# Carrying the sign of a double through a shift: one VectorE step fewer in the conversion of the weights, and new ranks for the planner

## Chip, core and metric

The kernel runs on one NeuronCore of a Trainium2 chip. The metric is the device time of one execution in microseconds (us), as the median of several runs.

Its engines are named as the profile names them: PE (TensorE, matmuls), PEld (PE's weight loads, which overlap its matmuls), DVE (VectorE), ACT (ScalarE), POOL (GpSimd) and SP (SyncE, here a queue that issues DMAs). Each works through its own instructions in the order in which the program was written, and waits on semaphores for the others.

## What is computed

The reference in its essence, for 4 batches, 8 heads, 576 positions, head size 64:

```python
scores = scale * q @ k.T
cum = np.cumsum(np.log(np.clip(f, 1e-4, 1.0)), axis=-1)
scores = np.where(causal, -1e9, scores + cum[:, :, :, None] - cum[:, :, None, :])
attn = softmax(scores) @ v                      # 4 x 8 heads of 576 x 64
x = attn.transpose(0, 2, 1, 3).reshape(2304, 512)
x = ((x @ w_a) * (x @ w_b)) @ w_out             # 512 -> 1536 -> 512
h = x @ w_in                                    # 512 -> 1024
solu = h * softmax(h)
out = (layer_norm(solu) * g_ln) @ w_out2        # 1024 -> 512
```

The weights of both MLPs and `g_ln` are float32 by value, but the conversion in the kernel shows how `moe_w_a`, `moe_w_b`, `moe_w_out`, `moe2_w_in` and `moe2_w_out` arrive: as 64-bit doubles, of which the kernel reads the two 32-bit halves and puts a float32 together by itself.

## The kernel before

**Precision.** PE multiplies a rounded type (fp32r). Every operand is split into a high part (a cast) and a low part (value minus high part), and a product is three matmuls: high by high, low by high, high by low. Casts and subtractions are what ACT, DVE and POOL mostly do.

**Stages.** Attention runs head by head (first the eight heads of batch 0 in two pieces each, then whole heads): transposes (L944), maxima of scores (matmul L1008, mask L1012, DVE's maximum L1032 or L1035), scores (L1082, L1090), exponentials on ACT (L1147, L1210), weighting with v (L1171, L1269), normalising (L1293 to L1325). Between them lie the "up" products (L1401: x by w_a and w_b, 1728 matmuls of 512 or 256 columns), whose results (ACT L1424, DVE L1426) go to DRAM through SP. When attention is over, the rest of the up products follow, then "down" (L1707: groups of 12 matmuls for one of 12 chunks, `down`), then pairs of 128 rows each (`pair`, `rest`): seven products of sums and differences (L1793), softmax and norm, transposes (L1902) and the last product (L1917). A block of down needs its chunk read back (nat), cast by ACT (L1695) and subtracted (L1699), with two buffers for it; when a block's four PSUM banks are full, ACT copies them out (L1716), and the next block may use them. For the first block these copies also have to come after the conversion of `moe2_w_in` (up to L1617 and L1621), whose memory they overwrite. The pair's quarters are then cast (L1757), subtracted (L1761) and combined (L1767).

**Conversion of a weight tile** (`load_cols`), 56 times, 48 of them with 512 columns and 8 with 256. A DMA brings both halves of the doubles into `raw`. Then:

1. L661: ACT (or POOL, L664) multiplies the high half, read as a float32, by 2^-112 (`rebias`).
2. L673 on ACT or L676 on POOL: the low half's top byte becomes the three missing mantissa bits (`three`).
3. L681 on DVE: shift the result of 1 left by three and OR in the three bits.
4. L685 on DVE: AND the high half with the sign bit and OR it in.
5. L690 on DVE for the 8 tiles of `moe2_w_out` alone: times `g_ln`.
6. L703 (ACT or POOL) casts the high part, L708 (DVE or POOL) subtracts for the low part; for `moe2_w_in` the tile goes through L1628 (differences), L1617 (casts) and L1621 (subtractions) first.

28 tiles (w_a, w_b) are converted while attention begins, 12 (`moe_w_out`) around its end, 8 (`moe2_w_in`) before the first pair and 8 (`moe2_w_out`) around it. In this kernel all 56 of step 1 stand on ACT.

**Order.** Nothing in it is written by hand. Every step is an operation with a key and one or two engines that can do it (`op`); `Sched.run` goes through them with a cost for each, gives out buffers and PSUM banks, picks for each engine the earliest that can start (by key among equals) and the engine that would end first, with a lean for each kind. The table `Y` holds the keys, ranks and leans. The list it makes is the program. Where the planner expects PE to be without work for more than `FG` us early in the kernel, `fill` (L1978) puts matmuls on PE whose results nobody uses, for the share `FF` of that gap.

Of the kernel before, what the change touches and what calls it, by code (L numbers as in the profile page):

```python
# [8 lines left out]
F32 = mybir.dt.float32  # L9
# [14 lines left out]
def t_act(n, psum=False):  # L24
    return (0.167 if psum else 0.2) + n / 1200.0


def t_dve(n):
    return 0.153 + n / 960.0
# [42 lines left out]
class Sched:  # L72
# [228 lines left out]
    "T0": 5.7779,  # L301
    "T1": 5.884,
    "TA": 10.92,
    "TF": 18.3671,
    "U0": 3.9329,
    "U1": 3.2704,
    "UF": 2.3238,
    "UL": 1.3336,
    "LEAD": (1.3468, 6.1224),
    "SHRINK": 2.3365,  # L310
    "W0": 39.835,
    "WD0": 3.1123,
    "WN": 4,
    "WD1": 0.0081,
    "WD2": 15.0328,
    "EZ": 9.4388,
    "EO": 19.7242,
    "TE": 28.8271,
    "DL": 0,
    "BIAS": 0.6613,  # L320
    "UO": (7.859, 9.2606, 7.5415),
    "UD": 27.1947,
    "UK": 414.1889,
    "L3": 17,
    "TL": (0.0, 0.0),
    "F1": 255.5172,
    "FG": 0.2449,
    "FF": 0.6945,
# [3 lines left out]
    "YC": 23.0831,  # L332
    "T2": 10.2775,
    "TB": 1,
    "HB": 1,
    "F2": 251.1376,
    "LATE": -0.663,
# [26 lines left out]
    "WIN": 0.0002,  # L364
# [4 lines left out]
def kernel(  # L369
# [228 lines left out]
    def load_cols(src_view, key, dst_hi, dst_lo, wbuf, wparts, tfetch=6.0, scale=None, kind=1,  # L598
# [35 lines left out]
        def wmv():  # L634
            return stage(wm, n)
# [13 lines left out]
        def hi_w():  # L649
# [6 lines left out]
        ab = op([("ACT", t_act(1.1 * n)), ("POOL", 0.18 + 0.00268 * n)], key - 0.6, None,  # L656
                r=[(raw, 0)], w=[(wm, 0)], lean="BA")

        def rebias():
            if ab.eng == "ACT":  # L660
                nc.scalar.activation(  # L661
# [890 lines left out]
    n = m = 0  # L1552
# [475 lines left out]
```

## Time and profile before

| | |
|---|---|
| median of 3 runs | 904.08 us (902.7 to 907.12) |
| the profiled execution: its time | 904.06 us |
| the profiled execution: its span in the trace | 902.3 us |
| PE busy | 886.6 us (98%) |
| DVE busy | 621.1 us (69%) |
| ACT busy | 456.4 us (51%) |
| POOL busy | 150.6 us (17%) |
| L661, L685 (steps 1 and 4 above) | 56 instructions each |

All durations below come from that profiled execution. Busy PE is not the same as useful PE: the filler of L1978 counts as busy, and matmuls are pipelined, so that a record lasts longer than the distance to the next. The chain of waits follows the work back from the last instruction, and each piece of it names what the end waited for at that moment.

### The profile page before, as it was taken

The page shows a single profiled execution, that of the slowest core. Times are in us where ns is not written, and L with a number is a line of the kernel's source. Part 1 is how long each engine was busy: PE and PEld are TensorE (multiplying, and loading weights), DVE is VectorE, ACT ScalarE, POOL GpSimd, SP SyncE. Part 2 cuts the span into 40 slices and gives each one's busy share as a digit, 9 for nine tenths or more (in the row PEclk, how much of TensorE's full clock was granted, in tenths as well). Part 3 has the DMA queues.
Part 4 walks back from the last instruction along what each step waited for, and adds up shares of the span by engine and source line. Part 5 has one row for each costly group of instructions (what it writes and reads, how often), then busy time and mean ns, then how long its engine had stood idle before and what let it go on. Part 6 is the DMA issues. An engine that isn't in the chain of part 4 may idle for free.

```text
span 902.3 us, 14146 instructions
## 1 busy us (share of the span) xinstructions
PE 886.6 (98%) x4968; PEld 758.8 (84%) x4973; DVE 621.1 (69%) x1214; ACT 456.4 (51%) x859; POOL 150.6 (17%) x293
## 2 busy tenths in 40 slices
PE   8999999999999999999999999899999999999997
PEld 5778878999888888888888889788888888888885
DVE  7877767677665567553773425889687678678775
ACT  5867766566556555454552324645334434253232
POOL 5766454243101111111110000000000000000000
PEclk9999999999999999999999999999999999999999
DMA  5465664334233333122563333442110111111101
GB/s 138 105 172 155 183 181 126 89 83 102 66 90 90 89 96 88 52 74 64 194 210 134 117 94 101 130 155 82 59 48 36 47 59 48 44 45 36 42 12 35
DMA packets 110042, 85.00 MB, mean 94 GB/s; under 512 B 69874, under 2 KB 91508, under 8 KB 109972
## 3 DMA queue, kind: packets, MB, share of 16 engines
q1 hardware_dynamic: 107652, 83.43, 32.3%
q10 hardware_dynamic: 2320, 0.68, 0.4%
q8 instruction: 39, 0.64, 0.3%
q14 instruction: 31, 0.25, 0.1%
HBM read 57.38 MB, written 19.55 MB: 85 GB/s over the span
## 4 chain that ended last, share of the span: by engine, by line
PE 92%; DVE 4%; ACT 1%; issue 1%; POOL 0%; DMA 0%; DVEq 0%; ACTq 0%; POOLq 0%
PE ps L1401 33%; PE ps L1707 16%; PE ps L1917 10%; PE ps L1793 9%; PE ps L1269 6%; PE ps L1090 3%; PE ps L1008 3%; PE ps L1171 3%; PE ps L1082 3%; PE ps L944 2%; PE ps L1902 2%; DVE mts L1032 1%; PE ps L1978 0%; PE ps L1050 0%; PE ps L1012 0%
## 5 line engine op out<-in xcount | busy, mean ns | idle before, releaser
L1401 PE MATMUL ps<-xs,wt 128*128 128x256 f32 (+1 forms) x1728 | 323.7, 340 | 0.1
L1401 PEld LDWEIGHTS ps<-xs,wt 128*128 128x128 f32 x1728 | 266.5, 189 | 33.4 <-POOL wt L708 0.5
L1707 PE MATMUL ps<-wt,sets 128*128 128x512 f32 (+1 forms) x420 | 91.0, 371 | 0.0
L1707 PEld LDWEIGHTS ps<-wt,sets 128*128 128x128 f32 x420 | 73.8, 190 | 13.4
L1793 PE MATMUL ps<-wt,xs 128*128 128x512 f32 x306 | 78.8, 394 | 2.6 <-ACT xs L1757 1.6
L1917 PE MATMUL ps<-wt 128*128 128x512 f32 x324 | 79.6, 394 | 1.5 <-ACT wt L1905 1.4
L1426 DVE TENSOR_TENSOR fw<-ps,fw 128x256 f32<-128x256 f32 (+1 forms) x72 | 40.0, 555 | 55.1 <-PE ps L1401 34.4
L1424 ACT COPY fw<-ps 128x256 f32<-128x256 f32 (+1 forms) x72 | 34.5, 479 | 83.3 <-PE ps L1401 80.9
L1917 PEld LDWEIGHTS ps<-wt 128*128 128x128 f32 x324 | 59.7, 188 | 14.7 <-ACT wt L1905 1.8
L1035 DVE CUSTOM_DVE_ANT_0 ps<-ps,cmask 128x512 f32<-128x512 f32 (+4 forms) x105 | 56.5, 555 | 22.1 <-PE ps L1008 19.6
L1793 PEld LDWEIGHTS ps<-wt,xs 128*128 128x128 f32 x306 | 57.4, 190 | 14.9 <-ACT xs L1757 1.8
L1695 ACT CAST wt<-nat 128x512 fp32r<-128x512 f32 (+1 forms) x60 | 34.6, 579 | 69.1 <-PE ps L1707 63.7
L1234 DVE TENSOR_TENSOR pexp<-fw,pexp 128x768 fp32r<-128x768 f32 (+1 forms) x44 | 45.2, 1027 | 33.3 <-ACT pexp L1228 32.6
L1699 DVE TENSOR_TENSOR wt<-nat,wt 128x512 fp32r<-128x512 f32 (+1 forms) x60 | 38.0, 635 | 40.9 <-ACT wt L1695 40.7
L1269 PE MATMUL ps<-pexp,VS 128*128 128x448 f32 (+4 forms) x396 | 64.8, 311 | 0.0
L1269 PEld LDWEIGHTS ps<-pexp,VS 128*128 128x128 f32 x396 | 59.5, 190 | 3.5
L1219 POOL TENSOR_SCALAR_AFFINE_SELECT fw<-fw 128x128 f32<-128x128 f32 (+1 forms) x120 | 34.5, 317 | 150.4 <-ACT fw L1210 150.4
L1082 PE MATMUL ps<-sets 128*128 128x320 f32 (+4 forms) x200 | 49.2, 295 | 0.1
L1210 ACT ACTIVATE fw<-ps 128x768 f32<-128x768 f32 (+1 forms) x48 | 39.6, 836 | 19.0 <-PE ps L1090 15.2
L1090 PE MATMUL ps<-sets 67*128 67x288 f32 (+6 forms) x200 | 48.9, 320 | 0.0
L1008 PE MATMUL ps<-sets 66*128 66x512 f32 (+3 forms) x192 | 44.3, 332 | 2.9 <-DVE mts L1032 1.1
L1293 ACT ACTIVATE xrw<-ps 64x576 f32<-64x576 f32 (+2 forms) x40 | 22.0, 550 | 48.1 <-PE ps L1269 37.8
(190 smaller groups left out, 1485.9 us busy)
## 6 DMA issues: line engine op xcount, KB each, us to landing
gs<-fw SPq DMA_DIRECT2D x36, 256.0 KB
nat<-gs SPq DMA_DIRECT2D x36, 256.0 KB
fw<-in_moe_w_out_dram SPq DMA_DIRECT2D x16, 512.0 KB
sets<-sets SPq DMA_DIRECT2D x48, 144.0 KB
fw<-in_moe_w_a_dram SPq DMA_DIRECT2D x10, 512.0 KB
fw<-in_moe_w_b_dram SPq DMA_DIRECT2D x10, 512.0 KB
gs<-fw SPq DMA_DIRECT2D x36, 128.0 KB
nat<-gs SPq DMA_DIRECT2D x36, 128.0 KB
```

Of the source, the lines that this page charges most:

```text
L1008: nc.tensor.matmul(bank(ms[part], o, w), lhsT=MB(st)[:D + 2, i * P:(i + 1) * P], rhs=SB(st)[:D + 2, k0:k0 + w], start=True, stop=not pm)
L1035: nc.vector.tensor_tensor_reduce(out=x, in0=x, in1=cmask[:n, off:off + w], scale=1.0, scalar=-3.0e38, op0=ALU.add, op1=ALU.max, accum_out= ...
L1082: nc.tensor.matmul(dst, lhsT=SA(st)[:, ks], rhs=MA(st)[:, q0:q1], start=True, stop=False)
L1090: nc.tensor.matmul(dst, lhsT=SB(st)[:depth, ks], rhs=MB(st)[:depth, q0:q1], start=False, stop=True)
L1210: op(("ACT", t_act(n, True)), key + K.rk[4] + 5.5 + 0.9 * i, lambda i=i, n=n, pf=pf: nc.scalar.activation(out=pf(), in_=bank(ss[i], K.base ...
L1234: o.fn = lambda o=o, bh=bh, bl=bl, n=n, pf=pf: ENG[o.eng].tensor_tensor(out=pexp[:, 64 * bl.slot:64 * bl.slot + n], in0=pf(), in1=pexp[:, ...
L1269: nc.tensor.matmul(bank(u, K.uo + q0, q1 - q0), lhsT=V[:, vp], rhs=src[:, o:o + q1 - q0], start=(k_ in K.first and ip == 0), stop=(k_ in K ...
L1401: nc.tensor.matmul(bank(u[m % len(u)], uo[m], n_), lhsT=wv(m, wp, c)[:, kk], rhs=xsv(i, xx, kk), start=(kk == 0 and n == 0), stop=(kk == K ...
L1426: op(("DVE", t_dve(n_)), key - 50.0, lambda: nc.vector.tensor_tensor(out=gtv(), in0=bank(u[-1], uo[1], n_), in1=atv(), op=ALU.mult), r=[(u ...
L1707: nc.tensor.matmul(bank(py, 512 * d, n), lhsT=WO[c][0][:, wp * DM:(wp + 1) * DM][:, ds_], rhs=ghv(gb, gp)[:, :n], start=(c == 0 and i == 0 ...
L1793: nc.tensor.matmul(bank(bk, 0, 512), lhsT=yc(yx, yp)[:, kk], rhs=wi(wx, wp, kk), start=(n == 0), stop=(n == 5))
L1917: nc.tensor.matmul(bank(po, 0, DM), lhsT=zp[:, c], rhs=w2(c, wp), start=(c == 0 and i == 0), stop=(c == NF2 - 1 and i == 2))
```

## The change

Step 4 is gone. Step 1 becomes an activation with a slope for negative numbers (`Prelu`, scale 2^-112, slope 2^32), on ACT alone: a negative number comes out 2^32 times larger, so that a bit stands in its exponent which step 3's shift by three moves into the sign. The choice of POOL for step 1 is no longer there.

Most numbers of the table `Y` are new. Two lists of PSUM banks for transposes (`pz`) and the last product (`po`) are cut or turned round.

```diff
-    "W0": 39.835,
+    "W0": 52.0369,
...
-    "PM": 11,
+    "PM": 10,
...
-        ab = op([("ACT", t_act(1.1 * n)), ("POOL", 0.18 + 0.00268 * n)], key - 0.6, None,
-                r=[(raw, 0)], w=[(wm, 0)], lean="BA")
-
-        def rebias():
-            if ab.eng == "ACT":
-                nc.scalar.activation(
-                    out=wmv(), in_=hi_w().bitcast(F32), func=AF.Copy, scale=2.0 ** -112)
-            else:
-                nc.gpsimd.tensor_scalar(
-                    out=wmv(), in0=hi_w().bitcast(F32), scalar1=2.0 ** -112, scalar2=None, op0=ALU.mult)
-
-        ab.fn = rebias
+        op(("ACT", t_act(1.1 * n)), key - 0.6, lambda: nc.scalar.activation(
+            out=wmv(), in_=hi_w().bitcast(F32), func=AF.Prelu, scale=2.0 ** -112, alpha=2.0 ** 32),
+           r=[(raw, 0)], w=[(wm, 0)])
...
-        op(("DVE", t_dve(n)), key + 0.03, lambda: nc.vector.scalar_tensor_tensor(
-            out=wmv().bitcast(I32), in0=hi_w(), scalar=-0x80000000, in1=wmv().bitcast(I32),
-            op0=ALU.bitwise_and, op1=ALU.bitwise_or), r=[(raw, 0), (raw, 1), (wm, 0)],
-           w=[(wm, 0)], port=True)
...
-            pz = s_.buf("pz", bank_at((7, 1), (6, 1), (5, 1), (4, 1)))
+            pz = s_.buf("pz", bank_at((7, 1), (5, 1), (4, 1)))
...
-        po = s_.buf("po", bank_at((7, 1), (6, 1)))
+        po = s_.buf("po", bank_at((6, 1), (7, 1)))
```

`W0` is the key from which the tiles of w_a and w_b are due; `PM` is the number of heads whose mask is a matmul (L1012) with a plain maximum on DVE (L1032), where the others add the mask on DVE (L1035).

In the listings below the new program's line numbers are smaller: step 1 is L656, what was L673 to L681 is L664 to L672, and from L690 on (which was L703) 13 are taken off.

**The first tiles of w_a and w_b, on DVE.** This stretch of DVE holds the end of the eight half-size heads of batch 0: splits of k and q (L967, L979), row maxima (L1032) and the normalising of finished heads (L1317, L1319, L1325). Before:

```order
L681 SCALAR_TENSOR_TENSOR fw<-fw 128x512
L1032 TENSOR_REDUCE mts<-ps 128x1 x4
L967 TENSOR_TENSOR sets<-ps,sets 64x256
L685 SCALAR_TENSOR_TENSOR fw<-fw 128x512
L1032 TENSOR_REDUCE mts<-ps 128x1 x2
L979 SCALAR_TENSOR_TENSOR sets<-ps,sets 64x256
L681 SCALAR_TENSOR_TENSOR fw<-fw 128x512
L1317 TENSOR_TENSOR xrw<-xrw 128x256
L1319 SCALAR_TENSOR_TENSOR xrw<-xrw 128x256
L967 TENSOR_TENSOR sets<-ps,sets 64x256
L1325 TENSOR_TENSOR xrw<-xrw 128x256
L979 SCALAR_TENSOR_TENSOR sets<-ps,sets 64x256
```
Now, in the same place:

```order
L966 SCALAR_TENSOR_TENSOR sets<-ps,sets 64x256 x2
L954 TENSOR_TENSOR sets<-ps,sets 64x256
L966 SCALAR_TENSOR_TENSOR sets<-ps,sets 64x256
L1019 TENSOR_REDUCE mts<-ps 128x1 x2
L1304 TENSOR_TENSOR xrw<-xrw 128x256
L1306 SCALAR_TENSOR_TENSOR xrw<-xrw 128x256
L954 TENSOR_TENSOR sets<-ps,sets 64x256
L1312 TENSOR_TENSOR xrw<-xrw 128x256
L966 SCALAR_TENSOR_TENSOR sets<-ps,sets 64x256
L966 SCALAR_TENSOR_TENSOR sets<-ps,sets 64x320
L954 TENSOR_TENSOR sets<-ps,sets 64x576
```
Steps 3 and 4 of the first tiles (L681, L685) stood among these; now no conversion is among them, and the first one (L672) comes eight rows further on, behind five more row maxima.

**Between the last up products and the first pair, on PE.** L1401 is up, L1707 down, L1793 the pair's products. Before:

```order
L1707 MATMUL ps<-wt,pexp 128x512 x36
L1401 MATMUL ps<-xs,wt 128x256 x228
L1793 MATMUL ps<-wt,xs 128x512 x6
L1707 MATMUL ps<-wt,sets 128x512 x24
L1793 MATMUL ps<-wt,xs 128x512 x14
L1793 MATMUL ps<-wt,sets 128x512
```
Now:

```order
L1694 MATMUL ps<-wt,pexp 128x512 x36
L1388 MATMUL ps<-xs,wt 128x256 x228
L1694 MATMUL ps<-wt,sets 128x512 x12
L1780 MATMUL ps<-wt,xs 128x512 x6
L1694 MATMUL ps<-wt,sets 128x512 x24
L1780 MATMUL ps<-wt,xs 128x512 x14
```
The first group of the second block of down (12 matmuls) has moved from behind the pair's first product to ahead of it.

**At the same place, on ACT.** L1424 empties the banks of an up product, L1716 those of the first block of down, L1757 is the pair's first cast, L1617 casts parts of `moe2_w_in`. Before:

```order
L1617 CAST wt<-xrw 128x512 x2
L1424 COPY fw<-ps 128x256
L661 ACTIVATE fw<-fw 128x512
L673 ACTIVATE fw<-fw 128x512
L1716 COPY xrw<-ps 128x512 x2
L1757 CAST xs<-xrw 128x256
L1716 COPY xrw<-ps 128x512 x2
```
Now:

```order
L1604 CAST wt<-xrw 128x512
L664 ACTIVATE fw<-fw 128x512
L656 ACTIVATE fw<-fw 128x512
L1703 COPY xrw<-ps 128x512 x2
L1411 COPY fw<-ps 128x256
L1744 CAST xs<-xrw 128x256
L1703 COPY xrw<-ps 128x512 x2
```
The first two copies (now L1703) have moved ahead of the last L1411.

**Late, on POOL.** Before, POOL's last conversion (L703) was also its last work. Now these follow it, all subtractions of two operands in SBUF, for down (L1686, which was L1699) and for pairs (L1748 and L1754, which were L1761 and L1767):

```order
L1686 TENSOR_TENSOR wt<-nat,wt 128x512
L1748 TENSOR_TENSOR xs<-xrw,xs 128x256
L1686 TENSOR_TENSOR wt<-nat,wt 128x512 x2
L1754 TENSOR_TENSOR xrw<-fw 128x256
L1754 TENSOR_TENSOR fw<-fw 128x2x128
L1686 TENSOR_TENSOR wt<-nat,wt 128x512
L1748 TENSOR_TENSOR xs<-fw,xs 128x256
L1686 TENSOR_TENSOR wt<-nat,wt 128x512
L1748 TENSOR_TENSOR xs<-fw,xs 128x256 x2
L1748 TENSOR_TENSOR VS<-fw,VS 128x256
L1686 TENSOR_TENSOR wt<-nat,wt 128x512 x3
L1754 TENSOR_TENSOR xrw<-xrw 128x256
```
These stood on DVE. In all it is 17 of L1686 (11 of 512 columns, 6 of 256), 8 of L1748 and 5 of L1754.

## Rows read from the trace of the kernel before

**Rows 1.** Page, section 1: busy us, share of span and instructions of each engine.
```profile
PE 886.6 (98%) x4968; PEld 758.8 (84%) x4973; DVE 621.1 (69%) x1214; ACT 456.4 (51%) x859; POOL 150.6 (17%) x293
```

**Rows 2.** Stretches: start:end, length, busy time of each engine, granted clock, DMA.
```profile
25.00:50.00 25.00, 24.60 (x182) 20.03 (x180) 22.04 (x36) 21.27 (x49) 17.96 (x26) 1.00 0.48 129
50.00:150.00 100.00, 97.52 (x661) 80.77 (x664) 72.47 (x126) 69.44 (x139) 56.61 (x77) 1.00 0.59 161
150.00:575.00 425.00, 424.74 (x2477) 378.73 (x2476) 260.08 (x494) 219.60 (x358) 59.16 (x141) 1.00 0.37 104
575.00:600.00 25.00, 22.64 (x92) 18.35 (x93) 20.34 (x40) 14.32 (x28) 0.62 (x1) 0.93 0.42 138
600.00:850.00 250.00, 250.00 (x1203) 209.23 (x1203) 191.64 (x394) 99.29 (x212) 1.49 (x2) 1.00 0.16 53
850.00:902.30 52.30, 46.07 (x238) 38.23 (x236) 35.43 (x79) 17.27 (x41) 0.00 (x0) 1.00 0.11 31
```

**Rows 3.** The same stretches, the filler products of L1978 alone.
```profile
25.00:50.00 25.00, 6.66 (x44) 4.00 (x44) 1.00 0.48 129
50.00:150.00 100.00, 7.02 (x24) 2.30 (x27) 1.00 0.59 161
```

**Rows 4.** Chain that ended last, 25 to 47 us: start, length, what.
```profile
26.46 0.23 PE ps L1978
...
33.44 1.40 issue
...
42.07 1.08 DVE fw L685
43.15 0.61 DVE fw L681
...
43.79 0.69 DVE fw L685
```

**Rows 5.** Timeline of DVE, 33 to 34 us: start, length, instruction, idle time before.
```profile
33.38 1.53 DVE L681 SCALAR_TENSOR_TENSOR fw<-fw 128x512 int32<-128x512 int32 x1 [1.19 <-POOL fw L676]
```

**Rows 6.** Timeline, 572 to 582 us: the joint of last up products and first pair.
```profile
572.30 1.89 DVE L1621 TENSOR_TENSOR wt<-xrw,wt 128x512 fp32r<-128x512 f32 x3
...
573.34 0.37 ACT L1424 COPY fw<-ps 128x256 f32<-128x256 f32 x1 [0.37 <-PE ps L1401]
...
574.74 1.06 ACT L1716 COPY xrw<-ps 128x512 f32<-128x512 f32 x2
...
576.29 0.73 PE L1793 MATMUL ps<-wt,xs 128*128 128x512 f32 x2 [1.55 <-ACT xs L1757]
...
578.10 2.07 PE L1793 MATMUL ps<-wt,xs 128*128 128x512 f32 x4 [1.07 <-DVE xs L1761]
```

**Rows 7.** Chain that ended last, 560 to 605 us.
```profile
559.99 14.20 PE ps L1401 x119
...
592.96 12.24 PE ps L1707 x54
```

**Rows 8.** Stretches of 2 us at the joint; the number after POOL is granted clock.
```profile
578.00:580.00 2.00, 1.90 (x5) 1.52 (x6) 2.00 (x7) 0.88 (x2) 0.00 (x0) 0.50 0.83 266
580.00:582.00 2.00, 2.00 (x8) 1.61 (x7) 1.52 (x5) 1.79 (x5) 0.00 (x0) 0.71 0.58 227
```

**Rows 9.** One line each: count, duration ns least/median/greatest, first and last start, forms.
```profile
L661 ACT ACTIVATE fw<-fw x44: 418/668/696, 20.4 to 605.0; 128x512 f32<-128x512 f32 x36, 128x256 f32<-128x256 f32 x8
...
L685 DVE SCALAR_TENSOR_TENSOR fw<-fw x44: 424/691/1650, 24.7 to 609.2; 128x512 int32<-128x512 int32 x36, 128x256 int32<-128x256 int32 x8
...
L708 POOL TENSOR_TENSOR wt<-fw,wt x28: 726/1277/1995, 26.3 to 147.1; 128x512 fp32r<-128x512 f32 x20, 128x256 fp32r<-128x256 f32 x8
...
L1699 DVE TENSOR_TENSOR wt<-nat,wt x60: 405/690/784, 511.2 to 857.6; 128x512 fp32r<-128x512 f32 x48, 128x256 fp32r<-128x256 f32 x12
```

**Rows 10.** Groups by form, ACT: busy, mean ns of one | idle before.
```profile
L1147 ACT ACTIVATE xrw<-ps 128x512 f32<-128x512 f32 x4 | 2.4, 594 | 0.1
```

**Rows 11.** Timeline of ACT, first microseconds.
```profile
0.80 1.28 ACT L442 ACT_TABLE_LOAD   x1 [0.80 <-PEq L2012]
```

More of the change, by code (lines that the diff above doesn't have):

```diff
@@ L300 @@
     "Z0": 8.6278,
[L301 to L309, printed above, removed]
+    "T0": 5.9385,
+    "T1": 5.8556,
+    "TA": 11.0841,
+    "TF": 17.4757,
+    "U0": 3.6574,
+    "U1": 3.0952,
+    "UF": 1.5426,
+    "UL": 1.2688,
+    "LEAD": (1.3363, 6.1224),
     "SHRINK": 2.3365,
-    "W0": 39.835,
+    "W0": 52.0369,
     "WD0": 3.1123,
     "WN": 4,
[L314 to L318, printed above, removed]
-    "DL": 0,
[L320 to L324, printed above, removed]
+    "WD1": 0.0741,
+    "WD2": 18.5478,
+    "EZ": 6.9647,
+    "EO": 22.3243,
+    "TE": 29.3126,
+    "DL": 0,
+    "BIAS": 0.6045,
+    "UO": (7.5408, 9.2606, 7.5415),
+    "UD": 12.2964,
+    "UK": 488.444,
+    "L3": 19,
     "TL": (0.0, 0.0),
-    "F1": 255.5172,
-    "FG": 0.2449,
-    "FF": 0.6945,
+    "F1": 209.5672,
+    "FG": 0.2923,
+    "FF": 0.8533,
     "RA": 1,
@@ L331 @@
     "HC": 2,
-    "YC": 23.0831,
-    "T2": 10.2775,
+    "YC": 19.9481,
+    "T2": 10.8153,
     "TB": 1,
-    "HB": 1,
-    "F2": 251.1376,
-    "LATE": -0.663,
+    "HB": 2,
+    "F2": 232.5795,
+    "LATE": 0.1132,
     "BH": 0.1497,
[7 rows of a table removed]
[7 rows of a table added]
     "XL": -0.4279,
[4 rows of a table removed]
[4 rows of a table added]
     "PO": 1,
[1 row of a table removed]
[1 row of a table added]
     "KE": 1,
@@ L362 @@
     "MX": -12.0368,
[1 row of a table removed]
-    "WIN": 0.0002,
[1 row of a table added]
+    "WIN": 0.0,
 }
```

24 rows, old and new, of the table Y are left out of this document.

## The prediction, made before the result was known

> **What bounds the kernel now.** I read the busy shares first [rows 1]: PE 98%, the others far less. A reader should not stop there, for two reasons: PE's filler counts as busy, and pipelined matmuls hide short pauses. So I next cut the span into stretches [rows 2] and set the filler beside them [rows 3]. From 150 to 575 us PE is busy 424.74 of 425, from 600 to 850 all of 250, with no filler. There nothing but PE's own work counts, and this change takes none of it away. What is not PE's work lies in four places. In 25 to 50 us PE is idle 0.40 and runs 6.66 of filler; in 50 to 150 it is idle 2.48 and runs 7.02 of filler; in 575 to 600 it is idle 2.36 at a granted clock of 0.93; in 850 to 902.3 it is idle 6.23, at the serial end of the last rows. The first 25 us hold the start, where no tile of a weight is on anyone's path yet. So of 902.3 us some 16.6 early, about 4 at the joint and 6.2 at the end can move at all.
>
> Then the chain of waits: who keeps PE waiting in those places? From 30 to 46 us it runs off PE, over DVE above all, and four of its pieces are conversion [rows 4]: 1.40 booked as issue, which is DVE's L681, 1.53 long after a wait of 1.19 for POOL [rows 5]; then L685 of 1.08, L681 of 0.61 and L685 of 0.69. At the joint PE ends its up products at 574.74 (576.29 less 1.55), waits 1.55 for ACT's cast, does two matmuls, waits 1.07 for DVE, and then runs at half clock [rows 6, 8].
>
> **The change part by part.**
>
> *Sign step gone.* 56 instructions L685, 48 of them at 0.69 us and 8 at 0.42 [rows 9], are 36.5 us of DVE's 621. None of this is time of the span by itself: beside a full PE (150 to 575, 600 to 850) it is hidden by PE's work and worth 0. It counts only where the chain goes through it, below. If the cover went, it would be a gain, not a cost.
>
> *Prelu for Copy on ACT.* 56 on ACT before and 56 after, so nothing changes engine. The trace has no Prelu. L661 takes 0.668 for 512 columns [rows 9], and another function of ACT over 512 columns 0.594 [rows 10]; L661 itself reaches 0.696. Between these ends Prelu costs 0.07 less to 0.03 more, 4 us less to 1.7 more of ACT in 56 instructions, hidden by an engine that is busy 51%; I take 0, since source and scale are L661's. What speaks against the change is a reload: a table load takes 1.28 us here [rows 11], and the order shows one load in either program, at the start, so its price is 0. The Trainium skill (ScalarE: Activation LUTs, "Table sets: the hidden batching unit") has a load wherever the next function is not in the active set; by it, and with the trace's 1.28 us, two loads for each of the first 28 tiles would be 72 us more on ACT. The order leaves that no chance.
>
> *Early stretch, 25 to 50 us.* The new keys put the tiles of w_a and w_b behind the last half-size heads on DVE. The four pieces above come off the chain there: 1.40 + 1.08 + 0.61 + 0.69 = 3.8 us. What is late next is PE's own up products, which now start later, and the row maxima; the order still has 15 fillers here where 43 stood, of 512 columns at 0.23 [rows 4], 3.4 us. So PE's 7.06 us of filler and idle can shrink by at most 3.7. I take 3.5. Bounds: 0 (another engine's wait takes the place) and 3.8.
>
> *50 to 150 us.* PE lacks work for 9.5 us in all [rows 2, 3]. DVE is the busiest of the others with 72 of 100 us, and L685 is some 14 of them (20 tiles at 0.69 and 8 at 0.42 [rows 9] are 17.2, less about five before 50 us); in return 10 of POOL's subtractions L708 go to DVE at 0.69, and the casts L703 of some tiles from ACT to POOL. The order keeps 23 fillers where 27 stood: 0.9 us less. With half of the 2.5 idle that makes 2.1; I take 2.0. Bounds: 0 and 9.5 - 23 x 0.23 = 4.2.
>
> *The joint.* Before, all four copies L1716 stood behind the last up result, behind two conversions on ACT, and the last subtraction of w_in (L1621) ended at 574.19 [rows 6]. With L685 gone from the tiles of w_in this ends earlier, and the order shows two of the copies ahead of the last up result and a group of down (12 matmuls) ahead of the pair's first product. The group needs its four banks: after L1424 (573.34 + 0.37) come one cast of 0.41 and two copies of 1.06 in all, so 575.2, about 0.45 after PE's last up product. Then it covers 12 x 12.24/54 = 2.7 us [rows 7], in which the pair's first operand is cast and subtracted. Before, PE lost 1.55 + 1.07 = 2.62 idle and, at a granted clock of 0.50 and 0.71 over two stretches of 2 us [rows 8], 1.0 + 0.6 of full-speed work, 4.2 in all. In [rows 2] no other stretch shows a clock below 1.00, and a pause of 0.45 is shorter than either of those two; so I take the clock as kept. Gain 4.2 - 0.45 = 3.7; bounds 0 (the copies come late as before) and 4.2.
>
> *One head fewer masked by matmul.* Five matmuls L1012 fewer and five maxima on DVE in the other form: a few tenths either way, 0.
>
> *Late subtractions on POOL.* 17 splits L1686 and 13 pair steps move from DVE, which is at 77% there [rows 2], to an idle POOL. A split costs 0.69 on DVE and 1.28 on POOL at the median, 2.0 at most [rows 9]. It is hidden by the group of 2.7 us that runs meanwhile from the other buffer: cast 0.6, then 1.3 makes 1.9. I take 0. Below nothing there is no room, PE being full. Above, see the second rival.
>
> *The end.* the last 19 rows of PE's order are the same in both programs, down to the counts: 0.
>
> The sum goes against the profiled execution's own 904.06 (span 902.30 and 1.76 around it; the median of the runs, 904.08, is the same): 904.06 - 3.5 - 2.0 - 3.7 = 894.9.
>
> **The rivals.**
>
> *Only the joint.* Early, the wait is not DVE's but ACT's or POOL's: ACT is at 69 of 100 us and POOL at 57 in 50 to 150 [rows 2], 21.27 of 25 for ACT before that, and the conversions moved out of the first stretch fall into the next. Then filler and idle come back as other waits: 904.06 - 3.7 = 900.4. For it speaks that up products, which used to fill gaps on PE from 27 us on, come later now; against it, that ACT and POOL both have less to do early by the order (fewer L703 on the one, fewer L708 on the other).
>
> *POOL's late splits hold PE up.* L681 on DVE took 1.53 instead of 0.69 when POOL was working [rows 5], and POOL's L708 up to 2.0 against a least 1.3 or so for this size [rows 9]: each seems to shut the other out. The late stretch had no work on POOL before; now it has 30 subtractions with both inputs in SBUF, amid DVE's own. A split of 0.6 + 2.0 is just the 2.7 of its cover; where DVE's lock adds another 0.7, PE waits 0.7. With all 17 so: 11.9, and 13 pair steps at 0.4 more, 5.2: 894.9 + 17.1 = 912.0. It decides from the point where cast and split take over 2.7. The Trainium skill (SBUF — State Buffer, "Who interferes with whom") says that a DVE instruction with two SBUF inputs and a GpSimd instruction that reads SBUF exclude each other for a whole instruction; the trace agrees with the 1.53. Against the rival: the same pairs ran side by side early with a median of 1.28, and pair steps are issued far ahead of their products.
>
> *It does not do what it says.* Prelu takes longer on ACT than Copy, or DVE's gain is eaten by the copies of results that it takes over from ACT (L1304, 11 more of 576 columns, most in the full stretch): nothing in the rows bears the first out, and the second is hidden by PE. Without any gain: 904.
>
> **How the numbers follow.** The forecast has a chance of 0.62. Its three terms all at their upper ends give 904.06 - 12.2 = 891.9, each at half of it 898.0; the runs reach 1.4 below their median, so I set its own range at 890.5 to 898.0. Only the joint, 900.4: 0.20. POOL's splits, 912: 0.08. No gain, 904: 0.10. The range reaches from 890.5 to the second case and the same 1.4 above it, 901.8; it leaves out the last two, 0.18. A measurement of this kernel tells about 0.5%, 4.5 us, from no change: faster than 899.5 is the forecast and half of the second case, 0.72; within it the rest of that and no gain, 0.20; slower than 908.6 the late splits, 0.08.
>
> **What would show it.** In the new profile: filler and idle of PE in 25 to 50 us down by 3 or more; the chain there with no conversion in it before the eighth half-size head is done; after the last up product a pause of PE under 0.6 and a granted clock of 1.00 in that stretch; L656 at 0.67; from there to the last 50 us PE idle below 1. I am wrong if PE waits for POOL's L1686, if the early idle time is the same under other names, or if the pause at the joint is still over 1.5.

## The result, and the profile after

The changed kernel takes 895.67 us (median of 4 runs, 895.35 to 895.8) where the kernel before took 904.35 in the same comparison: a ratio of 0.990, 95% interval 0.9876 to 0.9925. The forecast was 894.9. Below, "before" and "after" are these two kernels; the profiled execution of after took 895.35 us, with a span of 893.6.

Busy us of each engine after, for [rows 1]:

```profile
PE 881.0 (99%) x4931; PEld 754.2 (84%) x4939; DVE 592.9 (66%) x1147; ACT 429.6 (48%) x811; POOL 209.2 (23%) x357
```

DVE has lost 28 us, ACT 27, and POOL gained 59. PE lost 5.6 of busy time and 3.1 of idle time (15.7 of 902.3 before, 12.6 of 893.6 after), together the 8.7 by which the span fell. The stretches of [rows 2] after (start:end, length, busy time of PE, PEld, DVE, ACT, POOL, granted clock, DMA share, GB/s), and in the second fence filler alone, as in [rows 3]:

```profile
25.00:50.00 25.00, 23.70 (x164) 18.67 (x166) 20.38 (x38) 21.11 (x47) 15.87 (x27) 1.00 0.53 147
50.00:150.00 100.00, 98.78 (x681) 83.50 (x683) 66.87 (x123) 68.94 (x135) 51.08 (x79) 1.00 0.64 170
150.00:575.00 425.00, 424.88 (x2458) 377.95 (x2457) 254.13 (x481) 202.19 (x330) 90.82 (x170) 1.00 0.37 105
575.00:600.00 25.00, 25.00 (x111) 20.48 (x110) 21.66 (x37) 12.93 (x24) 5.77 (x6) 1.00 0.47 147
600.00:850.00 250.00, 249.78 (x1219) 209.27 (x1218) 186.62 (x368) 96.81 (x213) 31.80 (x29) 1.00 0.15 48
```

```profile
25.00:50.00 25.00, 4.36 (x14) 1.44 (x17) 1.00 0.53 147
50.00:150.00 100.00, 5.61 (x19) 1.85 (x23) 1.00 0.64 170
```

Filler and idle of PE in 25 to 50 us are 4.36 + 1.30 = 5.66, where they were 7.06; in 50 to 150 they are 5.61 + 1.22 = 6.83, where they were 9.5. The joint has no idle time at all (25.00 of 25), and its clock is 1.00.

A better measure than fixed stretches are two landmarks in PE's timeline that both programs have: the end of the last up product, and the start of the last transpose (L1902, now L1889). After, these are the two rows (564.77 + 4.96 = 569.73; before, the last transpose stands at 890.08):

```profile
564.77 4.96 PE L1388 MATMUL ps<-xs,wt 128*128 128x256 f32 x40
...
881.38 1.03 PE L1889 MATMUL ps<-ident,fw 128*128 128x128 f32 x8
```

| | up products end | from there to the last transpose |
|---|---|---|
| before | 574.74 | 315.34 |
| after | 569.73 | 311.65 |
| gained | 5.0 | 3.7 |

The two gains make 8.7, the difference of the spans. So nothing was gained or lost behind the last transpose, and the question is what made the 5.0 and the 3.7. The joint after, timeline (start, length, instruction, idle time before it in brackets), for [rows 6], and its granted clock in stretches of 2 us, for [rows 8]:

```profile
565.60 2.36 DVE L1608 TENSOR_TENSOR wt<-xrw,wt 128x512 fp32r<-128x512 f32 x3
...
567.99 1.07 ACT L1703 COPY xrw<-ps 128x512 f32<-128x512 f32 x2 [0.50 <-DVE wt L1608]
...
569.56 1.08 ACT L1703 COPY xrw<-ps 128x512 f32<-128x512 f32 x2
569.57 2.91 PE L1694 MATMUL ps<-wt,sets 128*128 128x512 f32 x12
```

```profile
568.00:570.00 2.00, 2.00 (x17) 1.95 (x16) 2.00 (x5) 2.00 (x5) 0.58 (x1) 1.00 0.25 66
570.00:572.00 2.00, 2.00 (x10) 1.64 (x9) 2.00 (x6) 1.35 (x4) 0.36 (x1) 1.00 0.96 309
```

ACT's first two copies (L1703) start at 567.99, as soon as the conversion of `moe2_w_in` has ended (L1608 at 565.60 + 2.36), and are over before ACT empties the last up product. PE's group of 12 (L1694) starts at 569.57, in the tail of the last up product, without a pause. It doesn't wait for the other two copies, which end at 570.64: its first six matmuls go to the first two banks. The pair's product (L1780) follows at 572.31.

Early, the chain of waits after (start, length, what), for [rows 4]:

```profile
30.14 0.53 ACT sets L951
...
32.25 0.67 ACT fw L664
...
33.72 0.92 DVE xrw L1312
...
35.48 0.53 PE ps L995 x2
```

No sign step and only one piece of conversion (L664, on ACT) is left in it before 45 us. In its place stand steps of attention, on ACT above all from 26.7 to 33.2 us and on DVE up to 35.4. From 35.48 on it runs over PE's own products nearly without a break: attention's, filler, and from 40.7 on up products among them.

### The profile page after: what moved, and what is told of

Its sections match the earlier page's. It is cut to its first block, busy times and chain, and to the rows that moved or that the text cites. A ratio compares the mean times of both kernels' runs of the same rounds, so it can differ in the third digit from the quotient of the medians.

```text
span 893.6 us, 14068 instructions
## 1 busy us (share of the span) xinstructions
PE 881.0 (99%) x4931; PEld 754.2 (84%) x4939; DVE 592.9 (66%) x1147; ACT 429.6 (48%) x811; POOL 209.2 (23%) x357
## 4 chain that ended last, share of the span: by engine, by line
PE 90%; DVE 5%; ACT 2%; DMA 1%; issue 1%; ACTq 0%; POOL 0%; DVEq 0%
PE ps L1388 33%; PE ps L1694 15%; PE ps L1904 9%; PE ps L1780 9%; PE ps L1256 7%; PE ps L1158 3%; PE ps L1077 3%; PE ps L995 3%; PE ps L1069 3%; PE ps L931 2%; PE ps L1889 1%; DVE cmask L1849 1%; PE ps L1965 1%; DMA fw<-in_moe_w_b_dram 0%; DVE mts L1019 0%
## 5 line engine op out<-in xcount | busy, mean ns | idle before, releaser
L1694 PE MATMUL ps<-wt,sets 128*128 128x512 f32 (+1 forms) x420 | 90.9, 370 | 0.0
L1694 PEld LDWEIGHTS ps<-wt,sets 128*128 128x128 f32 x420 | 73.1, 188 | 13.0
L1411 ACT COPY fw<-ps 128x256 f32<-128x256 f32 (+1 forms) x72 | 34.5, 479 | 94.2 <-PE ps L1388 91.5
L1780 PE MATMUL ps<-wt,xs 128*128 128x512 f32 x306 | 78.3, 393 | 0.1
L1022 DVE CUSTOM_DVE_ANT_0 ps<-ps,cmask 128x512 f32<-128x512 f32 (+4 forms) x110 | 59.0, 555 | 13.5 <-PE ps L995 10.8
L1780 PEld LDWEIGHTS ps<-wt,xs 128*128 128x128 f32 x306 | 56.5, 188 | 11.9 <-DVE xrw L1791 0.3
L1206 POOL TENSOR_SCALAR_AFFINE_SELECT fw<-fw 128x128 f32<-128x128 f32 (+1 forms) x120 | 36.7, 335 | 124.5 <-ACT fw L1197 124.3
L1221 DVE TENSOR_TENSOR pexp<-fw,pexp 128x768 fp32r<-128x768 f32 (+1 forms) x40 | 41.7, 1046 | 27.7 <-ACT pexp L1215 27.3
L1686 DVE TENSOR_TENSOR wt<-nat,wt 128x512 fp32r<-128x512 f32 (+1 forms) x43 | 28.6, 668 | 37.7 <-ACT wt L1682 37.5
L995 PE MATMUL ps<-sets 66*128 66x512 f32 (+2 forms) x192 | 44.2, 333 | 3.0 <-DVE sets L954 1.0
L1686 POOL TENSOR_TENSOR wt<-nat,wt 128x512 fp32r<-128x512 f32 (+1 forms) x17 | 23.0, 1354 | 101.6 <-ACT wt L1682 80.4
```

The lines of the kernel that those rows point to most:

```text
L995: nc.tensor.matmul(bank(ms[part], o, w), lhsT=MB(st)[:D + 2, i * P:(i + 1) * P], rhs=SB(st)[:D + 2, k0:k0 + w], start=True, stop=not pm)
L1022: nc.vector.tensor_tensor_reduce(out=x, in0=x, in1=cmask[:n, off:off + w], scale=1.0, scalar=-3.0e38, op0=ALU.add, op1=ALU.max, accum_out= ...
L1221: o.fn = lambda o=o, bh=bh, bl=bl, n=n, pf=pf: ENG[o.eng].tensor_tensor(out=pexp[:, 64 * bl.slot:64 * bl.slot + n], in0=pf(), in1=pexp[:, ...
L1686: o.fn = lambda o=o, gr=gr, gb=gb: ENG[o.eng].tensor_tensor(out=ghv(gb, 1)[:, :n], in0=grv(gr)[:, :n], in1=ghv(gb, 0)[:, :n].bitcast(F32), ...
L1694: nc.tensor.matmul(bank(py, 512 * d, n), lhsT=WO[c][0][:, wp * DM:(wp + 1) * DM][:, ds_], rhs=ghv(gb, gp)[:, :n], start=(c == 0 and i == 0 ...
L1780: nc.tensor.matmul(bank(bk, 0, 512), lhsT=yc(yx, yp)[:, kk], rhs=wi(wx, wp, kk), start=(n == 0), stop=(n == 5))
```

## The experiments

The kernels differ from before or after in a few lines, so line numbers shift by up to six; the text names the lines of after (or of before, where the kernel comes from it).

**The step alone, in the old order.** Before, in its own order of instructions, with the slope and without the 56 sign steps.

```diff
-                    out=wmv(), in_=hi_w().bitcast(F32), func=AF.Copy, scale=2.0 ** -112)
+                    out=wmv(), in_=hi_w().bitcast(F32), func=AF.Prelu, scale=2.0 ** -112, alpha=2.0 ** 32)
...
-        op(("DVE", t_dve(n)), key + 0.03, lambda: nc.vector.scalar_tensor_tensor(
-            out=wmv().bitcast(I32), in0=hi_w(), scalar=-0x80000000, in1=wmv().bitcast(I32),
-            op0=ALU.bitwise_and, op1=ALU.bitwise_or), r=[(raw, 0), (raw, 1), (wm, 0)],
+        op(("DVE", t_dve(n)), key + 0.03, lambda: None, r=[(raw, 0), (raw, 1), (wm, 0)],
```


> The kernel before, its order untouched on every engine, with the Prelu on ScalarE and the 56 sign steps on VectorE simply left away. Theory A (the step itself sits on the chain in places): early the chain of before holds two sign steps (1.08 and 0.69 us) and the joint one (0.70 us); without them 2 to 3 us early and about 1 us at the joint, where the copies still stand behind the last up result and the pause of 1.55 us stays: 904.35 - 3.5 = 900.8, between 899.5 and 902. Theory B (the gain is the new order's alone, the step is hidden everywhere): 904, within 1.

Measured: 899.84 us against 904.13 of before, ratio 0.9958 (0.9945 to 0.9971). The up products end at 572.44, 2.3 earlier than before; from there to the last transpose it is 313.21, 2.1 less. The joint, of ACT and PE (idle time and what ended it in brackets), and its stretches:

```profile
572.44 1.07 ACT L1714 COPY xrw<-ps 128x512 f32<-128x512 f32 x2
...
574.00 0.73 PE L1791 MATMUL ps<-wt,xs 128*128 128x512 f32 x2 [1.56 <-ACT xs L1755]
...
575.07 1.19 PE L1791 MATMUL ps<-wt,xs 128*128 128x512 f32 x4 [0.34 <-DVE xs L1759]
```

```profile
574.00:576.00 2.00, 1.66 (x6) 1.09 (x7) 1.99 (x6) 1.97 (x5) 0.00 (x0) 1.00 0.75 255
576.00:578.00 2.00, 2.00 (x11) 1.64 (x10) 1.93 (x7) 2.00 (x6) 0.00 (x0) 1.00 0.83 281
```

The first pause is the old one, 1.56 (its copies still stand behind the last up result, L1714 at 572.44). The second fell from 1.07 to 0.34, and the clock stayed at 1.00, in the stretch from 578 to 580 too, where before it fell to 0.50 and 0.71 [rows 8]. So the step alone is worth about half of the change, part of it by the clock.

**The order alone: all 56 steps back.** After, in its own order, with the sign step put back right behind the shift. The next four kernels are the same edit with another condition.

```diff
+        def shift():
+            nc.vector.scalar_tensor_tensor(
+                out=wmv().bitcast(I32), in0=wmv().bitcast(I32), scalar=3, in1=lo_w(),
+                op0=ALU.logical_shift_left, op1=ALU.bitwise_or)
+            if True:
+                nc.vector.scalar_tensor_tensor(
+                    out=wmv().bitcast(I32), in0=hi_w(), scalar=-0x80000000, in1=wmv().bitcast(I32),
+                    op0=ALU.bitwise_and, op1=ALU.bitwise_or)
```


> The changed kernel, its order untouched on every engine, with a sign step put back behind each of the 56 shifts (it writes what stands there already). Theory A: VectorE's 36 us come back in an order made without them: 2 to 3 us early, 2 to 4 at the joint, where the conversion of w_in ends later and the four banks come late: 895.67 + 5.5 = 901.2, between 899 and 903. Theory B (order alone): 895.7 to 897.

Measured: 905.0, ratio to before 1.0013 (1.0004 to 1.0022). The new order with the step in it is no better than the old one with it, and the 56 steps cost 9.3 us there where I had expected 5.5. The next four runs say where.

**Back for `moe2_w_in` alone (8 tiles).** The condition is now:

```diff
-            if True:
+            if whole is not None:
```


> The changed kernel, order untouched, with the sign step put back for the 8 tiles of w_in alone (5.5 us of VectorE between the end of attention and the joint). Theory A: the last subtraction of w_in, 567.96 us in the new trace, ends 2 to 2.8 us later, the copies of the four banks with it, TensorE pauses 1.5 to 2.5 us at the joint and the granted clock falls again: 895.67 + 3 = 898.7, between 897.5 and 899.9; up to the end of the up products nothing moves. Theory B: 895.7, within 0.5.

Measured: 896.1, +0.4 on after. I had expected 3. The timeline:

```profile
566.36 2.36 DVE L1614 TENSOR_TENSOR wt<-xrw,wt 128x512 fp32r<-128x512 f32 x3
...
568.75 1.07 ACT L1709 COPY xrw<-ps 128x512 f32<-128x512 f32 x2 [0.52 <-DVE wt L1614]
...
569.61 1.86 PE L1700 MATMUL ps<-wt,sets 128*128 128x512 f32 x7
```

The conversion (L1614 here) ends 0.75 later, and so do the first copies (568.75); but PE's group still starts at 569.61 without a pause. Of the 0.75 some 0.6 does reach the last transpose of this execution, all of it behind the joint (312.25 from the up products' end, against 311.65). So the end of the conversion is worth about half a microsecond, and is not what the 3.7 hang on.

**Back for w_a and w_b alone (28 tiles).**

```diff
-            if True:
+            if kind < 2:
```


> The changed kernel, order untouched, with the sign step put back for the 28 tiles of w_a and w_b alone (17 us of VectorE in the first 150 us). Theory A: the up products end 2 to 3 us later, the joint is as in the changed kernel: 895.67 + 2.5 = 898.2, between 897.2 and 899. Theory B (the early gain is of the order alone): 895.7, within 0.5. If the sign steps of w_a and w_b and those of w_in add up, this and the run with w_in alone together make the run with all of them, 5.5 us.

Measured: 900.86, +5.2. The up products end at 575.30, 5.6 later than after and later than before; behind them nothing changes (311.60). A stretch, and what PE waited for (total us, times, longest):

```profile
50.00:150.00 100.00, 96.76 (x654) 80.91 (x658) 80.91 (x143) 65.28 (x128) 49.79 (x74) 1.00 0.62 172
```

```profile
PE ps L1001 <- DVE sets L960: 2.1, 2, 1.1
...
PE ps L1001 <- DVE sets L972: 1.1, 2, 0.6
```

These 28 steps are 20 x 0.69 + 8 x 0.42 = 17.2 us of DVE. In the new order a third of that reaches PE: DVE is late with the splits of q and k (L954, L966; here L960, L972), and PE's matmuls for the maxima (L995, here L1001) wait for those, 3.2 us in all, where in after one such wait of 1.0 is left.

**Back for `moe_w_out` alone (12 tiles).**

```diff
-            if True:
+            if kind == 2 and whole is None and scale is None:
```


> The changed kernel in its own order, with the sign step put back for the 12 tiles of moe_w_out alone (converted around the end of attention, where PE is full). Theory A (hidden beside a full PE): 895.7 within 0.6, the last up product and the last transpose within 0.5 of the changed kernel's. Rival B (the 3.7 us that the runs so far leave over belongs to these): 898 to 899.5.

Measured: 896.96 (895.38 to 897.44). Its profiled execution is one at 897.44, and lost its 2 us at the start, far from these tiles: this is its stretch at 10 us, and then after's.

```profile
10.00:20.00 10.00, 8.27 (x49) 6.31 (x47) 5.35 (x16) 3.73 (x10) 4.91 (x21) 0.83 0.58 128
```

```profile
10.00:20.00 10.00, 8.29 (x58) 6.19 (x59) 6.00 (x19) 5.56 (x15) 4.49 (x18) 1.00 0.60 133
```

The granted clock is 0.83 there instead of 1.00, and the up products end 2.1 later; from there to the last transpose it is 311.65, as in after to the hundredth. Two executions with a mean clock of 0.999 (0.997 in the other four) took 895.4 and 895.5. PE's timeline is 1.8 behind that of after at 20 us and 2.1 at 137 us, and stays there to the end, while the 12 steps stand between 416 and 473 us, where PE is busy all the time. So the median is 1.3 above after's, but the steps of 0.69 have no part in that: they are hidden beside a full PE. Why four of six executions of this kernel have the lower clock, and none of the four of after, is not shown.

**Back for `moe2_w_out` alone (8 tiles).**

```diff
-            if True:
+            if scale is not None:
```


> The changed kernel in its own order, with the sign step put back right behind the shift for the 8 tiles of moe2_w_out alone (512 columns, 0.69 us each on DVE, around the first pair). Theory A (the joint's gain rests on these: DVE, whose subtraction the pair's second wait was for, no longer has the two steps of 0.69 in its way; steps put back for all 56 cost 3.7 us more than the sum of those for w_a, w_b and w_in): 898 to 899.5, PE waiting at the joint for a DVE instruction of the pair, and the granted clock below 1.00 behind it. Rival B (the 3.7 belongs to the 12 tiles of moe_w_out around the end of attention): 895.7 within 0.6.

Measured: 899.58 (899.25 to 899.81), +3.9. The up products end at 569.62, as in after; from there to the last transpose it is 315.91, 4.3 more. The first 80 us behind the up products, after and then this kernel, and what PE waited for there:

```profile
569.73:649.73 80.00, 79.89 (x366) 65.79 (x366) 69.75 (x135) 39.27 (x82) 16.28 (x16) 1.00 0.33 102
```

```profile
569.62:649.62 80.00, 77.25 (x342) 61.76 (x341) 72.68 (x133) 38.04 (x79) 17.59 (x16) 1.00 0.34 99
```

```profile
PE ps L1700 <- DVE wt L1692: 0.9, 2, 0.6
PE ps L1786 <- ACT xs L1750: 0.9, 1, 0.9
PE ps L1895 <- DVE cmask L1866: 0.6, 1, 0.6
```

```profile
579.62:589.62 10.00, 9.08 (x40) 7.10 (x39) 9.80 (x20) 3.62 (x7) 0.12 (x1) 1.00 0.45 129
...
599.62:609.62 10.00, 9.38 (x42) 7.70 (x42) 9.78 (x14) 5.05 (x11) 3.60 (x3) 1.00 0.27 79
```

These steps weigh as much as the whole gain behind the up products, but they do not bring back the joint's two pauses: PE starts its group without a pause, is idle 0.32 in the first 10 us, and loses most of the rest in the 40 us behind. Eight steps of 0.69 are 5.5 us, and 3.9 of them reach the end, while DVE is busy 9.7 of 10 us or more in four of the first five such stretches (8.1 to 9.6 in after): it converts these tiles, splits down's chunks (L1686, here L1692) and prepares the pair (L1754, L1748) at once. PE waits for its splits, and for ACT's cast (L1744, here L1750), which itself waited for DVE:

```profile
580.39 0.41 ACT L1750 CAST xs<-xrw 128x256 fp32r<-128x256 f32 x1 [0.89 <-DVE xrw L1760]
```

One thing I had expected did not come: the clock stayed at 1.00 all along. PE's loss here is idle time (2.75 of 80 against 0.11) and somewhat longer records.

The four groups add up: 5.2 + 0.4 + 0 + 3.9 = 9.5, and all together cost 9.3 (with the 0 of `moe_w_out` read from its timeline, and not its median).

**Only `moe2_w_out`, in the old order.** Before, with slope and without sign step for those 8 tiles.

```diff
-                    out=wmv(), in_=hi_w().bitcast(F32), func=AF.Copy, scale=2.0 ** -112)
+                    out=wmv(), in_=hi_w().bitcast(F32), func=AF.Prelu if scale is not None else AF.Copy,
+                    scale=2.0 ** -112, **({"alpha": 2.0 ** 32} if scale is not None else {}))
...
+        def sign():
+            if scale is not None:
+                return
```


> The kernel before in its own order, with slope and without sign step for the 8 tiles of moe2_w_out alone; the other 48 keep Copy and the sign step. Theory A (in the old order too the joint's second wait and the fall of the clock come from the two sign steps of 0.69 that stand on DVE between the pair's first products): the up products end at 574.7 as before, the first pause of 1.55 stays, the second of 1.07 falls to about 0.4, the clock stays at 1.00, and the time is 904.1 - 2.1 = 902.0 (901.4 to 902.8). Rival B (that gain came with the earlier steps or from elsewhere): 904.1 within 0.6.

Measured: 903.5 against 904.41, ratio 0.9986 (0.9975 to 0.9998). The joint on PE, and the clock:

```profile
576.61 0.73 PE L1799 MATMUL ps<-wt,xs 128*128 128x512 f32 x2 [1.55 <-ACT xs L1763]
...
577.69 2.04 PE L1799 MATMUL ps<-wt,xs 128*128 128x512 f32 x4 [0.34 <-DVE xs L1767]
```

```profile
578.00:580.00 2.00, 2.00 (x6) 1.52 (x6) 1.85 (x5) 1.34 (x4) 0.00 (x0) 0.50 0.97 356
580.00:582.00 2.00, 2.00 (x8) 1.61 (x7) 1.31 (x4) 1.89 (x5) 0.00 (x0) 0.71 0.27 111
```

The second pause fell to 0.34 as expected. The clock did not stay up: pauses of 1.55 and 0.34 as in the first experiment, but this time 0.50 and 0.71 behind them. So my reason for the clock was wrong, and the section on the hardware comes back to it. Without the clock (three executions at 1.000, 902.07 at the median, against 902.86 for 20 of before) the 8 steps are worth some 0.8 us in the old order, against 3.9 in the new one.

**The new ranks with the old step, planned anew.** Before's code with after's table and banks.

> The code of before with its sign step, and the new table of ranks and the two new lists of banks; the planner makes an order for it. Theory A (step and order belong together): the planner has 36 us more to place on VectorE, the ranks are not made for it: no gain, 904 to 910. Theory B (the ranks alone): near 896.

Measured: 920.68, ratio 1.0187 (1.0171 to 1.0203), beyond the 910 that I had expected at most. The ranks by themselves are worth nothing; given the step, the planner makes a poor program of them, in which the pair's first cast alone (L1757) keeps PE waiting 2.7.

**The late subtractions from POOL back to DVE.** After, with the 30 in their places in the order, but on DVE.

```diff
+    late_from = min(o.n for o in s_.users("y"))
+
     def emit(o):
+        if o.eng == "POOL" and o.n >= late_from:
+            o.eng = "DVE"
         now[:] = [o]
```


> The changed kernel, order by start untouched, with the 30 late subtractions that stand on GpSimd issued on VectorE in the same place. Tests whether they cost anything there. The prediction has 0 for them: 895.67, within 0.6. If GpSimd's splits hold TensorE up, or its lock stretches VectorE on the path (a subtraction of 0.42 us took up to 1.5 in the new trace), this is faster, 893 to 895. If VectorE was relieved by them, it is slower: 20 us more for VectorE in some 250, 896.5 to 898.

Measured: 896.45 (0.9917, 0.9902 to 0.9932). That is 0.8 over after, with intervals that overlap: POOL's late work costs nothing end to end, and if anything DVE's relief is worth a little (PE is idle 0.76 us from 600 to 850 here, 0.22 in after).

**ACT's first two copies behind the last up result**, as before had them, in after:

```diff
+    first = s_.queue["y"][0].users
+    ups = [o for o in s_.users("unit") if o.eng == "ACT"]
+    last = max(o.start for o in ups)
+    for x, o in enumerate([o for o in first if o.eng == "ACT"][:2]):
+        o.start = last + 1.0e-4 * (1 + x)
```


> The changed kernel with one thing undone at the joint: the first two copies of the first block's banks stand behind the last up result on ScalarE, as before; all else untouched. Theory A: these two copies start 1.4 us later (569.36 instead of 567.99 in the new trace), TensorE's group of 12 waits 0.8 to 1.0 us, no fall of the clock: 895.67 + 0.9 = 896.6. Theory B (ScalarE's order does not matter, the conversion's end does): 895.7, within 0.4.

Measured: 896.39 (0.9913, 0.9898 to 0.9929), +0.7. ACT's two copies start at 569.82 here, and PE at the joint shows:

```profile
570.47 2.83 PE L1694 MATMUL ps<-wt,sets 128*128 128x512 f32 x11 [0.19 <-ACT xrw L1703]
```

PE's group waits 0.19, and from the up products' end to the last transpose it is 0.8 more than in after; another half microsecond (the up products end at 570.27) was there before the joint. No run moves the group of 12 alone back behind the pair's first product, and none undoes the two lists of banks alone.

**No filler.** After without its 75 fillers, whose results nobody uses.

```diff
-    "FG": 0.2923,
+    "FG": 1.0e6,
```


> The changed kernel without its 75 filler matmuls, otherwise untouched on every engine. The sum of the prediction took filler and idle time as one, and fewer fillers as time gained. If that is right and the filler only stands in pauses, the pauses remain and the time is 895.7, within 0.7, as long as the granted clock stays at 1.00; where the clock falls in the first 130 us, the time rises by 3 us or more.

Measured: 902.39 (0.9979, 0.9968 to 0.999), 6.7 us slower than with filler. PE's timeline of this kernel, the same first row in after, and this kernel's stretches:

```profile
9.95 0.55 PE L995 MATMUL ps<-sets 66*128 66x256 f32 x1 [3.04 <-DMA sets<-xs]
...
36.62 0.85 PE L995 MATMUL ps<-sets 66*128 66x512 f32 x2 [2.28 <-DVE sets L954]
```

```profile
10.01 0.35 PE L995 MATMUL ps<-sets 66*128 66x256 f32 x1
```

```profile
30.00:40.00 10.00, 7.01 (x42) 5.71 (x42) 6.68 (x12) 7.78 (x19) 6.34 (x13) 0.79 0.27 61
40.00:50.00 10.00, 9.93 (x62) 8.20 (x59) 7.21 (x12) 7.22 (x15) 6.23 (x9) 0.87 0.44 129
```

At 10 us the same product of 256 columns takes 0.55 where it took 0.35, though the granted clock reads 1.00 for that stretch in both; PE is 1.7 behind at 19 us, of which it makes up 1.1 by 21 us, where after runs filler. After a pause of 2.28 for DVE's split (L954) the granted clock falls to 0.79 and 0.87, and at 45 us PE is 3.6 behind; at the end of the up products (574.92) it is 5.2. That is all that this execution lost: it took 900.62, and the median is 1.8 longer still. So taking work from PE that nobody needs made the kernel slower: what is left takes longer. I had taken the clock to stay, with 3 or more if it fell.

## Why the prediction was right, and where it was not

*Sign step gone, hidden beside a full PE.* Right for the 12 tiles of `moe_w_out` and nearly so for `moe2_w_in` (0 and 0.4 us put back). *It counts only where the chain goes through it*: right, and there it counted for w_a, w_b and `moe2_w_out`.

*Prelu for Copy.* Right: 668 ns at the median, as Copy took [rows 9].

```profile
L656 ACT ACTIVATE fw<-fw x44: 417/668/694, 33.5 to 592.2; 128x512 f32<-128x512 f32 x36, 128x256 f32<-128x256 f32 x8
```

*25 to 50 us, 3.5 taken.* This step failed in size: 1.4. The four pieces did leave the chain, as the chain after shows, and so did two more of the conversion, on POOL, that stood in the same chain of before and that I had not counted:

```profile
31.71 0.55 POOL wt L703
...
32.34 0.68 POOL fw L676
```

That is 5.0 us of chain gone, and 1.4 gained: I read what a chain piece is long as what its removal gives. The up products, which used to fill PE from 27 us on, now start at 40.4, and attention's steps took the place of the conversions in the chain (30.14 to 33.72). What was late next was, up to 35 us, not PE, as I had it, but ACT and DVE. The cap of 3.7 was mis-sized too. I had priced each filler at 0.23; but the fillers of before are of two sizes, all those of after of 512 columns, and the 14 records left in this stretch are 4.36 us, not 3.4:

```profile
L1978 PE MATMUL ps<-cmask,ident x92: 272/379/396, 5.7 to 133.3; 128*128 128x512 bf16 x53, 128*128 128x256 bf16 x39
```

*50 to 150 us, 2.0 taken.* Measured 2.7: idle time fell from 2.48 to 1.22, and filler from 7.02 to 5.61. *One head fewer masked by matmul*, taken as 0: the five matmuls were 1.1 us of PE, as the two rows show (before, then after; x and busy us):

```profile
L1012 PE MATMUL ps<-cmask,ident 128*128 128x128 bf16 (+1 forms) x55 | 12.0, 227 | 0.0
```

```profile
L999 PE MATMUL ps<-cmask,ident 128*128 128x128 bf16 (+1 forms) x50 | 10.9, 227 | 0.0
```

The two early terms were 5.5 in the sum and 5.0 in the trace. That they agree so well is luck, errors that cancel: 1.4 + 2.7 + 1.1, less 0.15 in the first 25 us, make 5.05.

*The joint, 3.7 taken.* Measured 3.7, with a partly wrong reason. What was lost there is what I had summed: the two pauses of 2.62 are gone, the clock is at 1.00, and the group of 12 covers the making of the pair's operands. But I hung it on the conversion of `moe2_w_in` ending earlier and on the copies, and the runs give these 0.4 and 0.7 when they are undone one at a time. The order by itself does not keep the 3.7 either, for DVE has no room behind the joint: with the eight sign steps of `moe2_w_out` back, up products to last transpose take 315.91, no less than before's 315.34, and the time is 3.9 more. I had the rows in view (the second pause was "for DVE") and did not ask which instructions stood on DVE then: L681 and L685 of these very tiles. What stays argued is which part of the new order takes the first pause away; the group of 12 ahead of the pair's product is the likely one, and no run moves it alone. The left-over pause of 0.45 was not there, since the group needs two of its four banks at first; about as much of the 4.2 went elsewhere behind the joint (0.22 of it idle time from 600 to 850), so that the 3.7 came out to the tenth is luck as well. And what I took as lost to the clock is lost in some executions only (below).

*Late subtractions on POOL, 0 taken, and their rival of 912.* The rival is refuted: the time is 895.67, and moved back to DVE these steps made the kernel no faster. POOL's 17 splits do take long, and DVE's pair steps do get held up, as the rival had it (after, after, before; ns least/median/greatest):

```profile
L1686 POOL TENSOR_TENSOR wt<-nat,wt x17: 732/1351/1827, 597.6 to 842.0; 128x512 fp32r<-128x512 f32 x11, 128x256 fp32r<-128x256 f32 x6
```

```profile
L1754 DVE TENSOR_TENSOR xrw<-xrw x18: 405/418/1507, 575.1 to 855.9; 128x256 f32<-128x256 f32 x18
```

```profile
L1767 DVE TENSOR_TENSOR xrw<-xrw x20: 417/420/428, 578.6 to 865.1; 128x256 f32<-128x256 f32 x20
```

A step of 0.42 takes up to 1.51 with POOL at work beside it, and in before, where POOL does next to nothing there, 0.43 at most; the four longest of all the steps L1754 (0.87 to 1.51) began 0.1 to 0.3 us behind an instruction of POOL. That two such instructions with both inputs in SBUF contend is what the Trainium skill says (SBUF — State Buffer, "Who interferes with whom"), and the trace agrees with it. But POOL is in none of PE's waits, for these operands are made far enough ahead.

*What was to show it.* Of the five signs three came: no pause after the last up product and a clock of 1.00, L656 at 0.67, and 0.22 of idle time from 600 to 850. The first, 3 or more off filler and idle time in 25 to 50, did not. The second came in part: the early chain was to have no conversion in it before the eighth half-size head is done, and one piece is left (on ACT, at 32.25).

*Only the joint (900.4)*, *no gain (904)*: both out. The first has a point: without the new order only 2.3 of the early 5.0 come.

What the change is worth, put together: the step taken out of the old order gives 4.3; the order with the step in it costs 0.9; both together give 8.7. (Between executions at a clock of 0.999 or more, which the last section explains, it is 3.2, 2.0 and 7.2.) The step is about half of the gain by itself, the order none of it by itself. The new order puts the instructions where they fit only if DVE has 36 us less to do: the same 56 steps cost 9.3 in it and 4.3 where they had come from.

## What to carry to other kernels

The length of a piece of the chain of waits is not yet what its removal gives (here 5.0 us of pieces gave 1.4): ask which instruction of another engine ends just behind it, and take what lies between the two. Work that is hidden in one order need not be hidden in another, so that a step that saves an engine time is worth measuring with the order made anew for it, and here the new order was worth nothing without it. Where an engine is the cover at a joint, list everything that stands on it there by tile, not just the instruction that the profile names as the one waited for.

## What the runs showed of the hardware

**The clock behind a pause falls in some executions and not in others.** Two programs with the same pauses at the joint, 1.56 + 0.34 and 1.55 + 0.34, had 1.00 throughout and 0.50, 0.71 behind it. The executions of one program show it too. Each run lists its mean granted clock: 20 executions of before at 1.000 took 902.86 at the median, 16 at 0.998 took 904.41, and 11 at 0.995 or 0.996 took 905.5 to 906.5. The 1.55 between the first two matches what the two stretches of [rows 8] cost, 1.6, in an execution at 0.998. In the first experiment four executions at 1.000 took 899.69 at the median and two at 0.997 took 901.28 and 901.39. All runs of after are at 0.999 or 1.000. So of the 8.7 some 1.6 is a fall of the clock that before has in more than half of the executions listed and that after, with no pause at the joint, did not show; compared at a clock of 0.999 or more, before stands at 902.9 and after at 895.7. What decides whether it falls in an execution is open. The Trainium skill (TensorE: Matmul & The Clock Gate, "What's actually happening") says that one kernel shows different numbers of slow matmuls at its start from run to run; no run here counts these at the start for one kernel, but the executions above show the like behind pauses in the middle of one.

**Filler is worth more than it takes.** 75 matmuls with no purpose, 20 us of PE's records, make this kernel 6.7 us faster. Without them matmuls ran slower both at the start, where the granted clock reads 1.00 all the same, and behind a pause of 2.28, where it reads 0.79. The first can be seen only in the length of equal matmuls, 0.55 against 0.35; why the column doesn't show it stays open.

**A record is not a price.** The 28 sign steps of w_a and w_b are 17.2 us of DVE and cost 5.2; 8 others are 5.5 us and cost 3.9; 12 are 8.3 us and cost nothing. What differs is how full DVE is and whether PE has work in hand: DVE is busy 67 to 81 of 100 us in 50 to 150, where PE itself lacks work; 9.7 of 10 behind the joint; and 60% in the long stretch from 150 to 575, where PE is full (17.9 of 25 from 450 to 475 with most of the 12 steps put back).
